# A two-part kernel, attention and a maxout feed-forward layer: its list of commands put in another order, with copies, casts and masks dealt to other engines

## The chip, the cores and the metric

The kernel runs on one core of a Trainium2 chip. The metric is device time in microseconds (us) of one execution. The core has a matrix engine (PE), a vector engine (DVE), an activation engine (ACT), a general one (POOL), and a fifth (SP) that here only issues transfers. Transfers go through 16 DMA engines, which the queues of SP, ACT and POOL share. In the profile, q0 carries what POOL issues, q1 what SP issues and q10 what ACT issues.

## The reference

Four batches, 8 heads, 768 positions, head size 64. Heads 0, 2 and 6 see all earlier positions ("far" heads); the other five see the first 4 positions and a window of 64 ("near" heads). The flags that say so are an input.

```
scores = q @ k.T / 8                      # (4, 8, 768, 768)
keep   = causal for heads 0, 2, 6; causal & (first 4 | last 64) for the others
a      = softmax(where(keep, scores, -1e9))
x      = (a @ v), heads side by side      # (3072, 512)
h      = max(x @ w1, x @ w2, x @ w3)      # 512 -> 768
out    = h @ w_out                        # 768 -> 512, fp32, (3072, 512)
```

All inputs are fp32; the kernel computes in fp16 and accumulates in fp32.

## The kernel before, in words

The kernel guesses the flags above, computes the fast path for them (`fast`, L154), compares the flags as it goes, and takes a general path at the end only if the guess was wrong or a sum is out of bounds.

The fast path has no loops over tiles. It is a list of commands, `PROGRAM` (L84), which the last lines of `fast` walk through in order, calling one small function for each. No scheduler reorders them: each engine gets its instructions in the order of the list and runs them in that order, waiting for others through semaphores. A command may put instructions on several engines. So the position of a command sets what stands behind what on each engine and on each queue, and a letter in it says which engine does its copy, cast or mask (a ACT, d DVE, p POOL, r a reduction on DVE) or which queue its transfer goes on (s SP, c or a ACT).

The stages of a batch, with their commands:

- **Batch 0 in.** Each half of 384 positions is loaded by pairs of heads: the first two pairs before the list begins, the rest by `hl half pair count queues` (L206, tiles `ks`, `qs`). `cast` turns k and q into fp16 (L220, `kn`, `qn`), `turnp` transposes them on PE (L238) and copies the result to `KQ` (L241). `load_v` loads v on SP's queue (L295 and L302, `vs`), `vc` casts it (L497), `vt` puts it in order by matmuls (L505) and copies it to `va` (L510). `kx0` and `y` copy the keys and values that near heads need beside the diagonal.
- **Batches 1 to 3 in.** `load b quad` loads k and q of four heads on POOL's queue (L257, `kq`), `turn` transposes them on DVE (L272). `load_v b half` on SP's queue, `v` and `y` cast v into place (L478, L524, L526).
- **Scores.** `s0` for batch 0 (L608), `s` for the others (L674): matmuls into a double bank `st`, then exponentials on ACT (L629, L691) to `pt`. `k0` and `k` multiply masks on (L377, POOL or DVE). A batch has 8 steps of `s`; they share two double banks.
- **Attention times v.** `av b half pair` (L717), reciprocal (L722) and product (L724) on DVE, then a transposing transfer on SP's queue (`D`, L730) or PE transposes and a copy (`x`, L740, L743) to `xT`.
- **Feed-forward.** `w 0` to `w 2` load w1 to w3 and `w 3` loads w_out, all on POOL's queue (L398, L393). `f b half wi ni` is one block of 128 of the 768 hidden columns with one of the three weights (L437, four matmuls): for wi 0 a copy to `acc` (L445), for wi 1 and 2 a maximum on DVE (L449). `o b half tb` is one block of 128 output rows (L462, six matmuls), a copy (L471) and a store (L472).
- **Others.** `gs` and `gp` are tiny transfers or copies that wait until something named has landed, and so hold back what is behind them on SP's queue or POOL. `idle` issues matmuls on zeros. `clear`, `cleark` fill constants. `flags`, `guess`, `check`, `verdict`, `read` compare the flags and sums and choose the path; `read` (L791) makes every engine load one value.

Buffers bound how far a command can run ahead: two of each tile of `hl` with two pairs, three `kq` tiles, three `vs` tiles, 17 tiles `pt`, four single and two double banks of PSUM.

The front of the list before, as far as POOL's and SP's queues go: on POOL `load 1 0`, `w 0`, `w 1`, `load 1 1`, `w 2`, `load 2 0`, each behind a number of copies and casts; on SP the k of `hl 0 2`, both halves of the first v, `hl 1 0`, `hl 1 2`, the second v.

The lines of `PROGRAM` that the prediction speaks of, before:

```
"turnp 1 0 dd, cast 1 3 dd, load 1 0, vt 0 02 da, cast 1 2 aa, vt 0 1 a, cast 1 1 pp",
"turnp 1 1 d, w 0, y 0 0 1:4:2 r p, s0 0 1 2, s0 0 1 3, y 0 0 4:5:1 r r, turnp 1 3 ad",
"turn 2 0 1 1, f 0 1 0 1 d, s 1 7, k 1 2 X 0 p, f 0 1 0 2 d, flags, load_v 1 0 s, v 1 0 0 d",
"w 3, v 1 0 2 d, f 0 1 1 2, s 1 3, f 0 1 2 2, f 0 1 1 1, load_v 1 1 s, k 1 3 Y 0 p, f 0 1 1 3",
"k 1 1 X 0 p, load_v 2 0 s, y 2 0 1:8:2 s a, f 0 1 1 5, f 0 1 2 5, y 1 1 1:8:2 r r",
```

Of the kernel before, what the change touches and what calls it, by code (L numbers as in the profile page):

```python
# [81 lines left out]
LEAST, MOST = 1.0e-9, 16.0  # L82

PROGRAM = (  # L84
# [65 lines left out]
)  # L150


# [889 lines left out]
```

## Time and profile before

| what | value |
|---|---|
| three runs | 192.91, 195.14, 195.88 us (median 195.14) |
| profiled execution, span | 195.2 us |
| PE busy | 180.9 us (93%) |
| DVE, ACT, POOL busy | 145.0, 98.8, 81.8 us |
| bytes moved | 26.59 MB |

The span runs from the first instruction to the end of the last transfer, and the profiled execution's own time is taken as that span. The shares are means over stages of different kinds: in the first third, where batch 0 is loaded and the scores of batch 0 and 1 are made, all engines and the transfers are busy; in the rest the feed-forward matmuls fill PE, and the others have room.

### The profile page before, as it was taken

How to read it: one execution, taken by the hardware profiler on the slowest of the kernel's cores; microseconds unless marked ns; L12 is line 12 of the kernel's file. 1: busy time of each engine (PE TensorE's matmuls, PEld its weight loads, DVE VectorE, ACT ScalarE, POOL GpSimd, SP SyncE). 2: the span in 40 equal slices, each digit the busy share in tenths (PEclk: the TensorE clock that was granted, in tenths of full speed). 3: DMA queues.
4: the chain of work that ended last, by engine and by line, in shares of the span. 5: the costliest groups of instructions: out<-in, count | busy, mean ns of one | idle time of the engine just before them, and what ended most of it. 6: DMA issues, size and time to landing. Idle time of an engine off the chain costs nothing.

```text
span 195.2 us, 4739 instructions
## 1 busy us (share of the span) xinstructions
PE 180.9 (93%) x1854; PEld 106.1 (54%) x1854; DVE 145.0 (74%) x308; ACT 98.8 (51%) x158; POOL 81.8 (42%) x140
## 2 busy tenths in 40 slices
PE   7896899998994899999999999999999999999990
PEld 2443646664562445675556565755665566565550
DVE  3758999987997393879897989857794689465541
ACT  3598797377944534679529532775434400211110
POOL 7595978819682296039705600332612500000000
PEclk9999999999999589999999999999999999999999
DMA  5999999999999647935969310241033012401413
GB/s 177 329 325 267 207 213 207 116 164 189 160 187 227 97 133 158 242 99 108 210 167 241 93 58 0 77 114 57 0 66 129 0 57 59 134 0 54 161 54 116
DMA packets 44248, 26.59 MB, mean 136 GB/s; under 512 B 31038, under 2 KB 39742, under 8 KB 44222
## 3 DMA queue, kind: packets, MB, share of 16 engines
q1 hardware_dynamic: 38798, 17.54, 36.8%
q0 software_dynamic: 4192, 7.87, 23.8%
q10 hardware_dynamic: 1232, 0.85, 1.4%
q8 instruction: 15, 0.25, 0.5%
q14 instruction: 11, 0.09, 0.1%
HBM read 25.17 MB, written 6.29 MB: 161 GB/s over the span
## 4 chain that ended last, share of the span: by engine, by line
PE 66%; DMA 12%; DVE 11%; SPq 5%; issue 2%; ACT 1%; ACTq 0%; DVEq 0%
PE yy L437 34%; PE yy L462 15%; DMA vs<-in_v_dram 8%; PE oacc L717 6%; PE st L674 5%; DMA qs<-in_q_dram 4%; SPq L302 4%; DVE KQ L272 4%; PE yst L437 3%; DVE x L724 2%; DVE acc L449 1%; PE yst L462 1%; DVE KQ L241 1%; SPq L283 1%; DVE vx L800 1%
## 5 line engine op out<-in xcount | busy, mean ns | idle before, releaser
L377 POOL TENSOR_TENSOR pt<-pt,kb 128x512 f16<-128x512 f16 (+5 forms) x53 | 48.3, 931 | 67.4 <-ACT pt L691 55.5
L691 ACT ACTIVATE pt<-st 128x1024 f16<-128x1024 f32 (+2 forms) x51 | 43.5, 908 | 24.6 <-PE st L674 24.2
L437 PE MATMUL yy<-xT,w2t 128*128 128x384 f16 x184 | 36.8, 330 | 0.0
L437 PE MATMUL yy<-xT,w0t 128*128 128x384 f16 x180 | 34.9, 326 | 0.6 <-DMA xT<-x 0.6
L437 PE MATMUL yy<-xT,w1t 128*128 128x384 f16 x176 | 34.4, 326 | 0.1
L462 PE MATMUL yy<-woutt,hT 128*128 128x512 f16 (+1 forms) x138 | 32.8, 384 | 0.0
L449 DVE TENSOR_TENSOR hT<-yy,acc 128x384 f16<-128x384 f32 x46 | 25.2, 555 | 6.8 <-PE yy L437 5.1
L449 DVE TENSOR_TENSOR acc<-yy,acc 128x384 f16<-128x384 f32 x44 | 24.0, 555 | 7.9 <-PE yy L437 4.0
L272 DVE STREAM_TRANSPOSE KQ<-kq 128x384 f32<-128x384 f32 x24 | 25.4, 1134 | 0.4 <-DMA kq<-in_q_dram 0.4
L437 PEld LDWEIGHTS <-w0t 128*128 128x128 f16 x192 | 18.1, 98 | 13.5 <-issue 1.7
L445 ACT CAST acc<-yy 128x384 f16<-128x384 f32 x27 | 12.9, 489 | 23.3 <-PE yy L437 21.2
L437 PEld LDWEIGHTS <-w1t 128*128 128x128 f16 x192 | 17.9, 98 | 12.3 <-issue 1.0
L437 PEld LDWEIGHTS <-w2t 128*128 128x128 f16 x192 | 17.8, 98 | 12.3 <-issue 0.9
L462 PEld LDWEIGHTS <-hT 128*128 128x128 f16 x150 | 14.8, 101 | 16.5 <-issue 2.0
L717 PE MATMUL oacc<-va,pt 128*128 128x65 f16 x392 | 19.1, 195 | 4.4 <-ACT va L478 3.5
L717 PEld LDWEIGHTS <-pt 128*128 128x128 f16 x472 | 17.6, 98 | 8.3 <-issue 4.4
L471 ACT COPY ot<-yy 128x512 f32<-128x512 f32 (+1 forms) x14 | 7.9, 566 | 23.6 <-PE yy L462 20.9
L724 DVE TENSOR_TENSOR x<-oacc,sums 128x384 f16<-128x384 f32 x32 | 17.8, 557 | 1.1
L629 ACT ACTIVATE pt<-st 128x1024 f16<-128x1024 f32 (+5 forms) x22 | 15.5, 760 | 3.1 <-PE st L608 2.9
L674 PE MATMUL st<-KQ 32*128 32x128 f16 (+2 forms) x342 | 15.3, 263 | 0.0
L377 DVE TENSOR_TENSOR pt<-pt,kb 128x256 f16<-128x256 f16 (+4 forms) x31 | 11.7, 383 | 1.8 <-ACT pt L691 1.7
L445 DVE CAST acc<-yy 128x384 f16<-128x384 f32 x18 | 10.0, 557 | 3.8 <-PE yy L437 3.3
(117 smaller groups left out, 187.6 us busy)
## 6 DMA issues: line engine op xcount, KB each, us to landing
out_dram<-ot SPq DMA_DIRECT2D x23, 256.0 KB, 2.2
vs<-in_v_dram SPq DMA_DIRECT2D x18, 256.0 KB, 6.0
ks<-in_k_dram SPq DMA_DIRECT2D x8, 192.0 KB, 5.1
kq<-in_k_dram POOLq DMA_DIRECT2D x3, 384.0 KB, 8.1
kq<-in_q_dram POOLq DMA_DIRECT2D x3, 384.0 KB, 9.2
kq<-in_k_dram POOLq DMA_DIRECT2D x3, 288.0 KB, 7.9
kq<-in_q_dram POOLq DMA_DIRECT2D x3, 288.0 KB, 10.0
qs<-in_q_dram ACTq DMA_DIRECT2D x4, 192.0 KB, 4.8
```

The costliest lines, as they stand in the source:

```text
L272: nc.vector.transpose(out=dst.rearrange("c (p j) -> c j p", j=n)[:, j0:j1], in_=src.rearrange("c (j i) -> c j i", i=R),)
L377: engine.tensor_tensor(out=x, in0=x, in1=of_blocks(kb, pattern, rows), op=ALU.mult)
L437: nc.tensor.matmul(yy[:, 0:HALF], w_t[wi][:, ks, ni * P : (ni + 1) * P], xT[b, half, ks].rearrange("p a t -> p (a t)"), start=(ks == 0), s ...
L445: op(out=acc[b, half, ni], in_=yy[:, 0:HALF])
L449: nc.vector.tensor_tensor(out=acc[b, half, ni] if wi == 1 else hT[b, half, ni], in0=yy[:, 0:HALF], in1=acc[b, half, ni], op=ALU.max,)
L462: nc.tensor.matmul(yo[:, 0:n], hT[b, half, ns][:, tb * P : (tb + 1) * P], woutt[:, ns, c : c + n], start=(ns == 0), stop=(ns == NNB - 1),)
L471: op(out=ot[:, c : c + n], in_=yo[:, 0:n])
L629: nc.scalar.activation(out=pts[0, half, hp, u][:, r0:r1, c0:c1], in_=sts[hp][:, r0:r1, c0:c1], func=AF.Exp, scale=sc,)
L674: nc.tensor.matmul(sts["XY"[g // 2]][:, g % 2, c0 : c0 + n * P], KQ[rows, 0, ki * P : (ki + 1) * P] if kind == "p" else kx[b % 2][quad][ro ...
L691: nc.scalar.activation(out=pts[b, s, xy][:, r0:r1, c0:c1], in_=st[:, r0:r1, c0:c1], func=AF.Exp, scale=sc,)
L717: nc.tensor.matmul(o[:, i, r, 0 : D + 1], at[b, h, kind, ki, qi], vv[:, 0 : D + 1], start=(n == 0), stop=(n == len(todo) - 1), skip_group_ ...
L724: nc.vector.tensor_tensor(out=x, in0=o[:, :, :, 0:D], in1=rc.unsqueeze(3).to_broadcast([P, HB, 2, D]), op=ALU.mult,)
```

## The change

Only `PROGRAM` changes. The same commands stand in another order, apart from the number of gates and idle matmuls, and in many of them the letter of the engine is another. The functions, tiles and buffers are untouched. What the prediction speaks of:

- POOL's first transfers: `load 1 0` stands behind the first cast, then `w 0`, `load 1 1`, `w 1`.
- SP's first transfers: `hl 0 2`, `hl 1 0`, the halves of the first v, the second v, and then `hl 1 2`.
- `load_v 1 1`, `1 0` and `2 0` and the gates that stood among them.
- `flags`, `guess`, `check`, `verdict` and `read` are near the end of the list.
- Letters: for instance the copies of `f` go from 28 on ACT and 20 on DVE to 31 and 17, the masks `k` from 43 on POOL and 29 on DVE to 45 and 27, copies of v (`v`) from 10 on ACT, 5 on DVE and 9 on POOL to 6, 4 and 10 and 4 reductions.

The front of the list, and the parts named (of 65 lines before and 68 after):

```diff
-    "idle 11, hl 0 2 2 sc, cast 0 1 pd, turnp 0 1 aa, cast 0 0 dd, cast 0 2 dp, load_v 0 0 0 4 s",
-    "load_v 0 0 4 4 s, turnp 0 0 ad, cast 0 3 pa, cleark 0 p, cleark 1 d, kx0 0 1 p, s0 0 1 1",
-    "s0 0 0 0, hl 1 0 2 ss, idle 1, turnp 0 3 da, turnp 0 2 da, s0 0 1 0, kx0 0 3 p, s0 0 0 3",
-    "vc 0 0 4 p, vc 0 4 4 p, s0 0 0 1, kx0 0 2 p, s0 0 0 2, hl 1 2 2 ss, cast 1 0 dd",
-    "turnp 1 0 dd, cast 1 3 dd, load 1 0, vt 0 02 da, cast 1 2 aa, vt 0 1 a, cast 1 1 pp",
-    "turnp 1 1 d, w 0, y 0 0 1:4:2 r p, s0 0 1 2, s0 0 1 3, y 0 0 4:5:1 r r, turnp 1 3 ad",
-    "s0 1 3 0, y 0 0 5:8:2 s r, clear 0 d, kx0 1 1 p, y 0 0 1:4:2 s p, s0 1 1 1, load_v 0 1 s",
-    "turnp 1 2 dd, kx0 1 2 r, av 0 0 1, s0 1 2 0, y 0 0 5:8:2 r r, kx0 1 3 r, w 1, gs 1, s0 1 0 1",
-    "av 0 0 0, av 0 0 3, s0 1 0 2, x 0 0 1 d, x 0 0 0 d, load 1 1, s0 1 3 2, vc 1 0 4 p",
+    "idle 11, cast 0 0 pd, load 1 0, hl 0 2 2 sc, turnp 0 0 aa, cast 0 3 dd, hl 1 0 2 ss",
+    "s0 0 0 0, w 0, cast 0 2 ap, load_v 0 0 0 4 s, turnp 0 2 ad, kx0 0 2 r, s0 0 1 2",
+    "cast 1 0 dd, cleark 0 p, turnp 0 3 da, load 1 1, turnp 1 0 ad, kx0 0 3 a",
+    "load_v 0 0 4 4 s, vc 0 4 4 d, vc 0 0 4 p, s0 0 0 3, s0 1 1 0, cast 0 1 pa, s0 1 0 0, w 1",
+    "load_v 0 1 s, vc 1 4 4 p, vt 0 1 a, s0 1 3 0, vt 0 02 da, y 0 0 1:4:2 s p, idle 1",
+    "vc 1 0 4 d, hl 1 2 2 ss, cast 1 2 ad, turnp 0 1 ad, vt 1 1 a, kx0 0 1 r, s0 0 1 3",
+    "cast 1 1 pp, turnp 1 1 a, cast 1 3 dd, s0 0 0 2, vt 1 02 da, y 0 0 4:5:1 s r, s0 0 1 0",
+    "turnp 1 2 ad, k0 0 0 2 d, y 0 1 1:4:2 r r, cleark 1 d, y 0 0 1:4:2 r d, y 0 0 4:5:1 r p",
+    "k0 0 3 2 d, y 0 0 5:8:2 s p, w 2, y 0 0 5:8:2 r a, s0 0 0 1, kx0 1 2 r, s0 0 1 1",
...
-    "k 1 1 X 0 p, load_v 2 0 s, y 2 0 1:8:2 s a, f 0 1 1 5, f 0 1 2 5, y 1 1 1:8:2 r r",
...
+    "k0 3 0 2 p, s 1 1, av 0 1 2 D, f 0 0 1 4, load_v 1 1 s, av 0 1 3, k 1 1 X 1 p, f 0 0 2 4",
+    "y 1 1 4:5:1 r p, s 1 2, k 1 2 X 1 p, k 1 1 Y 0 d, f 0 0 2 2, turn 2 0 0 0, x 0 1 3 a",
+    "f 0 0 2 1, k 1 2 X 0 d, f 0 0 2 5, s 1 3, k 1 3 X 0 p, f 0 1 0 5 a, f 0 1 1 5, clear 1 p",
+    "turn 2 0 1 1, load_v 1 0 s, y 1 1 1:8:2 r p, turn 2 0 0 1, kx 2 0 p, f 0 1 0 1 a",
+    "f 0 1 0 2 a, s 1 5, k 1 5 X 1 p, f 0 1 0 0 d, f 0 1 0 3 a, f 0 1 1 0, v 1 0 1 a",
+    "k 1 0 X 0 p, k 1 1 X 0 p, s 1 7, y 1 0 4:5:1 s p, f 0 1 2 0, k 1 5 X 0 p, w 3, f 0 1 1 1",
...
+    "load_v 2 0 s, v 2 0 1 a, f 0 1 2 4, v 2 0 0 p, gp 1 2, f 0 1 2 5, f 0 1 2 1, v 1 1 0 r",
...
+    "f 3 1 2 3, guess, verdict, f 3 1 1 1, f 3 1 2 1, o 3 0 0 a, f 3 1 2 4, f 3 1 2 5",
+    "o 3 1 1 d, o 3 1 0 d, o 3 1 2 a, read",
```

105 rows, old and new, of the table PROGRAM are left out of this document.

## The prediction

> **What bounds the kernel now.** I read the page first (busy shares, slices, the chain), then the table by stretches, then the chain in order of time, then the DMA queues of a few stretches.
>
> ```profile
> span 195.2 us, 4739 instructions
> PE 180.9 (93%) x1854; PEld 106.1 (54%) x1854; DVE 145.0 (74%) x308; ACT 98.8 (51%) x158; POOL 81.8 (42%) x140
> PEclk9999999999999589999999999999999999999999
> PE 66%; DMA 12%; DVE 11%; SPq 5%; issue 2%; ACT 1%; ACTq 0%; DVEq 0%
> 5.50:57.00 51.50, 46.49 (x554) 27.62 (x554) 44.66 (x90) 39.27 (x65) 37.60 (x72) 1.00 1.15 214
> 60.00:72.00 12.00, 8.50 (x65) 4.48 (x63) 7.73 (x14) 5.96 (x8) 4.87 (x8) 0.72 0.73 136
> 72.00:190.00 118.00, 118.00 (x1182) 70.15 (x1180) 87.18 (x189) 51.84 (x82) 32.68 (x45) 1.00 0.39 98
> ```
>
> The columns of a stretch are its length, then busy time of PE, PEld, DVE, ACT and POOL, then clock, DMA share and GB/s. From 72 to 190 PE has no gap at full clock. That part can only begin earlier or later: the change rearranges PE's work and takes none away. So a gain or a loss must lie in the first 72 us, and it has two places: 5 us missing of 51.5 in the front, and the hole at 60 to 72, which also halves the clock (the 5 in the slices).
>
> ```profile
> 51.10 10.15 DMA vs<-in_v_dram
> 61.28 1.04 ACT L526 CAST vx<-vs 64x1024 f16<-64x1024 f32 x1 [4.45 <-DMA vs<-in_v_dram]
> 64.17 0.65 PE L717 MATMUL oacc<-va,pt 128*128 128x65 f16 x9 [3.50 <-ACT va L478]
> ```
>
> The hole: a v transfer lands at 61.25, ACT, which takes its commands in order, is stuck 4.45 us at the cast that needs it, and PE waits 3.5 us for ACT's next cast of v. PE's mean clock over 60 to 72 is 0.72, which costs 12 x 0.28 = 3.4 us more, some of it beside the idle time: about 6.3 us in all.
>
> Why that v is late, and what the change could do to the front, is read from the queues (q0 carries what POOL issues, q1 what SP issues).
>
> ```profile
> q0 software_dynamic: 584, 0.60, 89.9%
> q1 hardware_dynamic: 572, 0.15, 27.6%
> vs<-in_v_dram SPq DMA_DIRECT2D x1, 256.0 KB, 15.7
> ...
> q0 software_dynamic: 336, 0.81, 104.6%
> q1 hardware_dynamic: 26, 0.02, 1.7%
> ...
> q1 hardware_dynamic: 680, 0.49, 110.4%
> ```
>
> The first three rows are 54 to 58 us, the next two 17 to 21, the last 12 to 13.5. Alone, SP's queue passes 680 packets in 1.5 us, 453 per us. When POOL's queue has work too (54 to 58), the two pass packets one for one, 584 to 572: SP's queue falls to 143 packets per us, a third, because POOL's packets are long. That is the wait on w 3 and `load 2 0`, and the 15.7 us of that v.
>
> **The change part by part.**
>
> *Engine shares.* Copies, casts and masks go to other engines, but by the durations of before's rows the sums stay: DVE 157.7 to 157.8 us, ACT 110.5 to 110.0, POOL 81.6 to 80.8, as I added them command by command. I take 0; in the stretch that is all PE they have room (DVE 87 of 118).
>
> *The v loads of batches 1 and 2.* The gates on SP's queue go to late places, `load_v 1 1`, `1 0` and `2 0` come one behind the other, and `w 3` behind the first two. The hole should not come back at this place: -6.3 us. If it does, the price is the same 6.3.
>
> *The tail.* `check`, `verdict`, `guess` and `read` move to the end. PE's last matmul ends at 190.50 and the span at 195.2; the 4.7 us are the last copy, store and its landing. `read` costs each engine one load of 0.3 to 0.6 us beside that: 0 to 0.6, I take 0.
>
> ```profile
> 190.50 0.03 ACTq L471
> L791 SPq TENSOR_LOAD <-differ x1: 592/592/592, 168.0 to 168.0; - x1
> ```
>
> *The front.* Here is the large term. Before, POOL issues `load 1 0` at 12.20, `w 0` at 14.44, `w 1` at 18.59 and `load 1 1` up to 21.4.
>
> ```profile
> 4.95 0.50 POOL L220 CAST kn<-ks 128x384 f16<-128x384 f32 x1 [0.54 <-DMA ks<-in_k_dram]
> ...
> 12.20 0.75 POOL L257 DMA_DIRECT2D kq<-in_k_dram  x1
> ...
> 18.59 0.75 POOL L398 DMA_DIRECT2D w1t<-in_moe_w_dram  x1
> ...
> 20.37 1.00 POOL L257 DMA_DIRECT2D kq<-in_q_dram  x2
> ...
> q0 software_dynamic: 34, 0.10, 52.6%
> kq<-in_q_dram POOLq DMA_DIRECT2D x1, 288.0 KB, 12.7
> 15.65 0.55 DVE L220 CAST qn<-qs 128x384 f16<-128x384 f32 x1 [0.59 <-DMA qs<-in_q_dram]
> ```
>
> The 34 packets are the whole of q0 in 16 to 17, and none came ahead of 16.2. So before, all of batch 0's q, k and v went out first with the DMA engines to itself (the last q is there at 15.65, SP's queue is all but empty at 17: 26 packets in 17 to 21), and the four POOL pieces ran behind it, from 16.2 to about 33.6 (the last issue at some 20.9 plus 12.7): 4.35 us each. After, `load 1 0` stands right behind the first cast (4.95 to 5.45), `w 0` and `load 1 1` follow with little before them, `w 1` behind the first cast of v; and SP's queue has the last q and k of batch 0 (`hl 1 2 2`) at its end, behind all of v. With one packet for one, whatever POOL's queue holds goes ahead of the end of SP's: from 8.9 (issue at 4.9 plus the 4.0 us from 12.20 to 16.2), SP's queue has 453 x (17.0 - 8.9) = 3670 packets left, POOL's four pieces some 1680 (the page has 4192 packets for ten such pieces).
>
> ```profile
> q0 software_dynamic: 4192, 7.87, 23.8%
> ```
>
> 3670 is over 1680, so all four pieces pass first and each sets the end of SP's queue back by its own 4.35 us: 17.0 + 4 x 4.35 = 34.4 for the last of `hl 1 2 2`, where its time without them is 17.0. The first of its four transfers lands some 1.8 us before (three quarters of 0.79 MB at 327 GB/s, the rate of the 12 to 13.5 stretch): 32.6. When POOL's queue starts hardly matters, as long as it starts before SP's is empty. `w 1` is the least sure: it waits for the first half of v, which is held back too (there at about 26), and it still goes ahead if SP's queue has over 420 packets left by then, which it has (3670 - 1257 = 2413 at the end of the third piece, 5.3 us alone, less some 3.5 us for v, its cast and the issue: about 815).
>
> What hangs on `hl 1 2 2`: ACT casts its first k in order, and everything of ACT stands behind it.
>
> ```profile
> L629 ACT ACTIVATE pt<-st 128x1024 f16<-128x1024 f32 (+5 forms) x22 | 15.5, 760 | 3.1 <-PE st L608 2.9
> L691 ACT ACTIVATE pt<-st 128x1024 f16<-128x1024 f32 x39 | 38.3, 1021 | 20.1 <-PE st L674 19.9
> ```
>
> From that cast up to `s 1 2`, ACT has 15 of batch 0's 22 exponentials (10.7 us), 6 of batch 1's (6 x 1.02 = 6.1) and 20 casts and copies (11.1), 27.9 us. DVE has 27 there, so ACT sets it. The last two exponentials are behind PE's part, so PE is through `s 1 2` at 32.6 + 27.9 - 2.0 = 58.5. Then PE's own work is left: 131 hidden blocks, 24 output blocks, 21 score steps and three batches of attention times v.
>
> ```profile
> 111.39 8.45 PE yy L437 x52
> 178.80 3.88 PE yy L462 x18
> 121.13 0.56 PE st L674 x12
> 123.47 1.31 PE oacc L717 x42
> ```
>
> Four matmuls are a hidden block: 8.45 / 13 = 0.65, 131 x 0.65 = 85.2. Six are an output block: 3.88 / 3 = 1.29, 24 x 1.29 = 31.1. Score steps 21 x 0.565 = 11.9. Attention 118 matmuls a batch, 3 x 118 x 0.031 = 11.0. Together 139.2. With 2.0 for short waits and the tail's 4.7, the **sum is 58.5 + 139.2 + 2.0 + 4.7 = 204.4**. It is made against the profiled 195.2, which stands on the median, 195.14. In general, with n POOL pieces ahead of `hl 1 2 2`, the time is 187.0 + 4.35 n. I take n = 4 and round to 204. The waits, 2.0, I don't see in the trace: 0 if DVE and POOL never lag, 5 (what PE lacks of 51.5 in before's front) if they do as before.
>
> ```profile
> 12.00:14.00 2.00, 2.00 (x25) 1.23 (x26) 1.08 (x4) 1.91 (x3) 1.95 (x6) 1.00 1.09 324
> ```
>
> The 4.0 us from 12.20 to 16.2 are the one thing that speaks for another start. In those 4 us DVE ran casts of fp32, up to 16.20. The Trainium skill, SBUF — State Buffer, "🔬 SBUF: two separate sides", says that a POOL-issued transfer's descriptors can't be written while DVE runs a copy in its two-port mode, fp32 copies above all. By that rule the start would be at the end of DVE's early casts, some 9.5 in after, which would leave the sum as it is and take the ground from rival B; the trace agrees in the one start at 16.2, but DVE was busy for only 1.08 of the 2 us from 12 to 14, so it doesn't prove it.
>
> **The rivals.**
>
> *B, faster, n = 0 to 1.* POOL's queue gets going only as SP's runs dry. For it: before's first POOL packet comes at 16.2, just as SP's queue empties. Against it: at 54 to 58 the two queues do share, while SP's was far from empty. What decides: whether POOL's packets start before 15 or not. Then `hl 1 2 2` is there at 15.2 to 17, the front runs as in before or better, and the hole at 61 is gone: 187.0 to 191.4, I take 189. It checks from the other end: 195.2 less the 6.3 of the hole is 188.9.
>
> *C, no change, n = 2.* POOL's queue shares but starts late (after 12) or runs dry, since `load 1 1` and `w 1` stand behind casts of data that is itself held back; two pieces go ahead: 195.7. The gain of the hole and the loss in front are then about equal. For it: `w 1` hangs on v; against it: nothing holds `load 1 0` and `w 0`, and `load 1 1` waits only for the cast of a q on the first loads.
>
> *D, slower by less, n = 3.* `w 1` comes too late to go ahead: 200.1.
>
> *E, slower by more.* As forecast, and the hole comes back with some other v: 204.4 + 6.3 = 210.7. Against it: the v loads have no gate and no weight in their way.
>
> **How the numbers follow.** Forecast (n = 4) 0.38, own range 201 to 208; D 0.12; B 0.28; C 0.18; E 0.04. Faster by over 2% (below 191.2) is B, 0.28. Slower by over 2% (above 199.0) is the forecast, D and E less a little, since D lies on the bound: 0.52. Within 2%, about what a measurement of this kernel tells from no change: 0.20. The range of 8 in 10 goes from B's middle to the top of the forecast, 188 to 208.
>
> **What would show it.** Right: in the stretch 8 to 26, q0 and q1 have equal packet counts and the GB/s that SP's queue moves fall to a fifth; the cast of batch 0's last q is past 30 (15.65 before); PE's slices from 12 to 33 us show low digits and the clock falls; no wait of ACT for v at 61; PE solid from 58 to 199. Wrong: q0 without packets before 15 (B); the last cast at 24 to 26 (C) or near 29 (D). The forecast also falls if PE, though late, has less than 139 us left then, because other blocks were done in the wait: the order on PE is fixed, so I hold that for unlikely.

## The result, and the profile after

The changed kernel takes **226.7 us** (median of five runs, 223.7 to 228.7) against 195.1 for before (median of five, 191.4 to 200.3). The ratio is **1.17, 95% interval 1.148 to 1.193**. The forecast had the sign and not the size: 204.

Both kernels have some longer executions, the profiled ones of before (span 195.2) and after (span 226.9) among them, and every ratio here is made between the others, where before takes 190.2 to 191.0 us on the chips of the experiments.

Where a difference in us is given below, the ratio is multiplied by about 190.4. The changed kernel is then at 222.9, and its interval alone runs from 218.6 to 227.2. A run's time is 1.7 to 2.1 us longer than its span. The prediction's sum is one of spans.

The page of the changed kernel:

```profile
span 226.9 us, 4743 instructions
PE 189.1 (83%) x1854; PEld 108.5 (48%) x1854; DVE 155.1 (68%) x302; ACT 99.8 (44%) x162; POOL 81.4 (36%) x142
PE   7405296899999858759995999999999999999980
PEclk9955569799999988958999799999999999999996
PE 52%; DVE 17%; DMA 16%; SPq 5%; ACT 4%; issue 3%; DVEq 0%; ACTq 0%
```

PEld is PE's loading of weights. Each of the 40 slices is 5.7 us. PE has three weak places. The first is the front (slices 2 to 5, 6 to 28 us, with the clock at half from slice 3 on), the second runs from slice 14 to 18 (74 to 102 us) with the clock down again, the third is slice 22 (119 to 125 us). DVE, which had 11% of the chain before, has 17% now.

The front, first the queues from 12 to 16 us, then the casts of batch 0's v and of its last keys and queries, then PE at `s 1 2` (line numbers are 3 higher than before):

```profile
q0 software_dynamic: 379, 0.62, 84.0%
q1 hardware_dynamic: 377, 0.27, 27.6%
```

```profile
25.16 0.82 POOL L500 CAST vn<-vs 128x768 f16<-128x768 f32 x1 [14.23 <-DMA vs<-in_v_dram]
...
30.67 0.51 ACT L223 CAST kn<-ks 128x384 f16<-128x384 f32 x1
...
32.88 0.55 DVE L223 CAST qn<-qs 128x384 f16<-128x384 f32 x1
...
59.47 0.22 PE L677 MATMUL st<-KQ 32*128 32x128 f16 x4
```

One packet for one, 379 to 377, as the prediction read it from 54 to 58 us of before. POOL gets its first v at 25.2 (forecast: about 26), ACT's first cast of the last k is at 30.7 (32.6), the last q is cast at 32.9 (34.4), and `s 1 2` ends on PE at 59.7 (58.5). In these numbers the forecast holds within 2 us. The way there is another one, as the queues from 25 to 30 us, q1 from 30 to 36 and two pieces of the chain show:

```profile
q1 hardware_dynamic: 1747, 1.28, 85.4%
q0 software_dynamic: 123, 0.19, 24.6%
...
q1 hardware_dynamic: 11, 0.01, 0.4%
...
8.23 18.07 DMA vs<-in_v_dram
26.33 0.57 DVE vn L500
```

POOL issues `w 1` at 26.38, and by 30, when SP's queue has 11 packets left, only 123 packets of POOL's queue have passed, of some 420 in a piece. So three pieces went ahead of SP's queue and the fourth came too late, as in rival D. The chain runs through the v transfer, and no piece of it is a transfer of `hl 1 2 2`.

Behind it, by stretches (length, busy PE, PEld, DVE, ACT, POOL, clock, DMA share, GB/s), and the pieces of the chain in the weak place:

```profile
59.70:220.40 160.70, 149.20 (x1426) 86.28 (x1426) 122.82 (x229) 65.65 (x100) 53.10 (x93) 0.96 0.47 102
80.00:99.00 19.00, 11.78 (x127) 6.35 (x123) 17.08 (x21) 4.15 (x6) 10.50 (x16) 0.86 0.92 165
```

```profile
81.97 7.51 DVE pt L380
...
92.55 6.40 DMA xT<-x
```

PE's last matmul ends at 220.4, that is 160.7 us after `s 1 2`, where the forecast had 139.2 and 2.0 for waits. PE stands idle for 11.5 us of these, and the other 10.0 above 139.2 are in its busy time, at a mean clock of 0.96. In 80 to 99 alone PE is busy for 11.8 of 19 us. The chain goes through one DVE instruction of 7.51 us. The timelines of DVE and of POOL show what it is:

```profile
81.42 0.56 DVE L727 TENSOR_TENSOR x<-oacc,sums 128x384 f16<-128x384 f32 x1
81.89 7.60 DVE L380 TENSOR_TENSOR pt<-pt,kb 128x128 f16<-128x128 f16 x1
89.41 0.18 DVE L725 RECIPROCAL sums<-oacc 128x6 f32<-128x6 f32 x1
...
118.00 4.11 DVE L380 TENSOR_TENSOR pt<-pt,kb 128x1024 f16<-128x1024 f16 x2
```

```profile
80.02 3.50 POOL L380 TENSOR_TENSOR pt<-pt,kb 128x512 f16<-128x512 f16 x4
83.47 0.49 POOL L481 CAST va<-vs 128x384 f16<-128x384 f32 x1
83.93 1.77 POOL L380 TENSOR_TENSOR pt<-pt,kb 128x256 f16<-128x256 f16 x2
85.66 0.94 POOL L481 CAST va<-vs 128x384 f16<-128x384 f32 x2
86.57 2.39 POOL L380 TENSOR_TENSOR pt<-pt,kb 128x256 f16<-128x256 f16 x3
88.92 0.49 POOL L481 CAST va<-vs 128x384 f16<-128x384 f32 x1
```

A mask of 128x128 (`k 1 4 X 0`), 0.23 us elsewhere, takes 7.60 us and ends at 89.49, just as POOL's row of masks and casts ends at 89.41. The same again at 118: the first of the two masks (`k 2 2 Y 0`) lasts 3.85 us, until 0.6 us after POOL's next row ends. Before the row at 80 us POOL stood still at a copy of v, and its work then comes without a gap (read from the trace, not tried by itself). It also issues `w 3` late, and PE waits for w_out:

```profile
67.68 0.29 POOL L527 CAST vx<-vs 64x128 f16<-64x128 f32 x1 [8.67 <-DMA vs<-in_v_dram]
...
82.95 2.33 PE L465 MATMUL yy<-woutt,hT 128*128 128x512 f16 x6 [2.53 <-DMA woutt<-in_moe_w_out_dram]
```

So there were three theories of the 32 us: the late front, the long masks, and the order behind the front as such.

### The profile page after: what moved, and what is told of

Read it like the earlier page. It is cut to its first block, busy times and chain, and to the rows that moved or that the text cites. A ratio compares the mean times of both kernels' runs of the same rounds, so it can differ in the third digit from the quotient of the medians.

```text
span 226.9 us, 4743 instructions
## 1 busy us (share of the span) xinstructions
PE 189.1 (83%) x1854; PEld 108.5 (48%) x1854; DVE 155.1 (68%) x302; ACT 99.8 (44%) x162; POOL 81.4 (36%) x142
## 4 chain that ended last, share of the span: by engine, by line
PE 52%; DVE 17%; DMA 16%; SPq 5%; ACT 4%; issue 3%; DVEq 0%; ACTq 0%
PE yy L440 27%; PE yy L465 10%; DMA vs<-in_v_dram 10%; DVE pt L380 6%; DMA xT<-x 4%; SPq L305 4%; PE st L677 3%; PE oacc L720 3%; DVE x L727 3%; PE yst L440 3%; DMA ks<-in_k_dram 2%; DVE hT L452 2%; DVE acc L452 2%; PE vb L508 2%; ACT pt L632 1%
## 5 line engine op out<-in xcount | busy, mean ns | idle before, releaser
L380 POOL TENSOR_TENSOR pt<-pt,kb 128x256 f16<-128x256 f16 (+5 forms) x53 | 46.5, 896 | 53.0 <-ACT pt L694 42.6
L465 PE MATMUL yy<-woutt,hT 128*128 128x512 f16 (+1 forms) x138 | 34.1, 393 | 4.7 <-DMA woutt<-in_moe_w_out_dram 2.5
L440 PE MATMUL yy<-xT,w1t 128*128 128x384 f16 x184 | 36.9, 331 | 0.0
L440 PE MATMUL yy<-xT,w2t 128*128 128x384 f16 x184 | 36.0, 326 | 0.7 <-DVE hT L452 0.5
L452 DVE TENSOR_TENSOR acc<-yy,acc 128x384 f16<-128x384 f32 x46 | 25.2, 554 | 14.8 <-PE yy L440 11.9
L474 ACT COPY ot<-yy 128x512 f32<-128x512 f32 (+1 forms) x16 | 9.1, 566 | 49.7 <-PE yy L465 35.5
L380 DVE TENSOR_TENSOR pt<-pt,kb 128x512 f16<-128x512 f16 (+5 forms) x31 | 25.1, 823 | 3.9 <-ACT pt L694 3.8
L440 PEld LDWEIGHTS <-w0t 128*128 128x128 f16 x192 | 18.0, 99 | 17.1 <-DMA xT<-x 4.1
L720 PEld LDWEIGHTS <-pt 128*128 128x128 f16 x472 | 19.1, 101 | 7.4 <-issue 1.7
L720 PE MATMUL oacc<-va,pt 128*128 128x65 f16 x392 | 20.9, 199 | 1.8 <-DVE pt L380 1.5
L677 PEld LDWEIGHTS <-KQ 32*128 32x128 f16 x342 | 9.3, 95 | 7.7 <-issue 6.6
```

Of the source, the lines that this page charges most:

```text
L380: engine.tensor_tensor(out=x, in0=x, in1=of_blocks(kb, pattern, rows), op=ALU.mult)
L440: nc.tensor.matmul(yy[:, 0:HALF], w_t[wi][:, ks, ni * P : (ni + 1) * P], xT[b, half, ks].rearrange("p a t -> p (a t)"), start=(ks == 0), s ...
L452: nc.vector.tensor_tensor(out=acc[b, half, ni] if wi == 1 else hT[b, half, ni], in0=yy[:, 0:HALF], in1=acc[b, half, ni], op=ALU.max,)
L465: nc.tensor.matmul(yo[:, 0:n], hT[b, half, ns][:, tb * P : (tb + 1) * P], woutt[:, ns, c : c + n], start=(ns == 0), stop=(ns == NNB - 1),)
L474: op(out=ot[:, c : c + n], in_=yo[:, 0:n])
L677: nc.tensor.matmul(sts["XY"[g // 2]][:, g % 2, c0 : c0 + n * P], KQ[rows, 0, ki * P : (ki + 1) * P] if kind == "p" else kx[b % 2][quad][ro ...
```

## The experiments

**The front, taken out and put in alone.** In the changed kernel, POOL's four first loads were moved behind its last cast of batch 0:

```diff
-cast 0 0 pd, load 1 0, ...   s0 0 0 0, w 0, ...   turnp 0 3 da, load 1 1, ...   s0 1 0 0, w 1
+cast 1 1 pp, load 1 0, w 0, load 1 1, w 1
```

> The changed kernel with one part undone: load 1 0, w 0, load 1 1 and w 1 stand behind the last cast that POOL does of batch 0 (cast 1 1), so that batch 0's q, k and v have the queues to themselves. Theory (POOL's early loads starve batch 0): the first cast of the last k is back from 30.67 to 16 to 18 us, PE is through s 1 2 at 43 to 46 instead of 59.7, and the time falls by 13 to 16 us to 208 to 212; more, down to 192, if the waits of PE between 70 and 128 were a consequence of the late front. Rival (the order of the list itself is bad and the loads are hidden): under 4 us gained, 219 or more.

Measured: 214.4 us, ratio 1.126 (1.123 to 1.129). The last q is cast at 20.2, and all behind it comes 11 us sooner, the 7.6 us mask as well (at 71.0 now). The gain is 8.5 us from 222.9. That is less than the front costs by itself (17.1, in h2_front_of_after below). A wait that the edit makes of its own, 3.1 us on PE, is a part of the difference. The rest stays open.

The reverse, in the kernel before:

```diff
-cast 1 3 dd, load 1 0, ...   turnp 1 1 d, w 0, ...   kx0 1 3 r, w 1, ...   x 0 0 0 d, load 1 1
+cast 0 1 pd, load 1 0, ...   cleark 0 p, load 1 1, ...   s0 0 0 0, w 0, ...   vc 0 0 4 p, w 1
```

> The kernel before with that part alone: load 1 0 behind the first cast, load 1 1 and w 0 a few commands on, w 1 behind the first cast of v. Theory: three to four pieces of 4.35 us go ahead of hl 1 2, the last k and q of batch 0 are cast at 28 to 33 instead of 15.65, and the time is 205 to 212. Rival (the starved data is not what the front hangs on, or the queues don't share there): 193 to 198, or a little faster since batch 1 is there sooner.

Measured: 207.5 us, ratio 1.090 (1.083 to 1.096), **17.1 us** more. The queues from 20 to 26 us, and the last q:

```profile
q0 software_dynamic: 616, 0.92, 84.0%
q1 hardware_dynamic: 617, 0.45, 30.3%
...
31.50 0.55 DVE L223 CAST qn<-qs 128x384 f16<-128x384 f32 x1 [1.18 <-DMA qs<-in_q_dram]
```

It is 15.85 us later than the 15.65 of before. Here `w 1` is issued at 14.46, so that all four pieces go ahead, and the time is close to the forecast's 4 x 4.35 = 17.4. With two of the four pieces:

```diff
-cast 1 3 dd, load 1 0, ...   turnp 1 1 d, w 0
+cast 0 1 pd, load 1 0, w 0
```

> The kernel before with only load 1 0 and w 0 moved to the front, w 1 and load 1 1 where they were. The prediction's price of 4.35 us for each piece ahead of hl 1 2: two pieces, so 8.7 us over before, and the last q of batch 0 cast at 24 instead of 15.65. If the price isn't per piece (a fixed loss once POOL's queue has begun), 15 us or more; if the two fit in beside SP's queue, under 3.

Measured: ratio 1.039 (1.026 to 1.051), 7.4 us more, the last q at 22.76. The price is by the piece.

**The two long masks.** Two letters of the changed kernel:

```diff
-k 1 4 X 0 d   k 2 2 Y 0 d
+k 1 4 X 0 p   k 2 2 Y 0 p
```

> The changed kernel with two letters changed: the masks k 1 4 X 0 and k 2 2 Y 0, which took 7.60 and 3.8 us on DVE while POOL ran without a gap, go to POOL. Theory (DVE's masks are locked out by POOL's run): DVE has 7.3 and 3.2 us back, the two holes of PE at 83 to 99 and 118 to 127 shrink, and 5 to 9 us are gained, 216 to 220. Rival (POOL's own queue of masks and casts of v sets the end there anyway): under 2 us, 223 to 226.

Measured: ratio 1.129 (1.123 to 1.135), some **8 us** less than the changed kernel (about 4 us either way, by the two intervals). No DVE mask is over 1.7 us there, and PE has 15.69 busy us from 80 to 99 where it had 11.78. But at the second place a DVE copy of keys (`kx`, 128x512, 0.28 us elsewhere) now takes 2.99 us.

```profile
80.00:99.00 19.00, 15.69 (x185) 9.28 (x185) 11.96 (x25) 8.58 (x13) 11.66 (x18) 0.91 1.00 176
```

**Both.** The edits of e1_pool_late and e3_two_masks together:

> The changed kernel with both undone: POOL's first loads late as in e1_pool_late, and the two masks on POOL as in e3_two_masks. If the two costs are separate, they add: 214.4 less some 8, so 205 to 208. If the masks only matter in the starved schedule: 213 to 215.

Measured: 206.9 us, ratio 1.078 (1.062 to 1.093): they add, 17.7 us under the changed kernel by the ratios, for 8.5 and 8 of the two alone. But 15 us over before are left, and a third mask takes 3.55 us. It is the one of 128x384, `k 2 1 X 0`. (The expectations of e10_spaced_w3 and h3_front_of_before_masks call it `k 2 3 Y 0`, which is a mask of 128x256 and takes 0.46 us here.) Part of the rest is the edit's own: POOL issues loads in a row from 19.2 on, the second transfer of the last one (`load 2 0`) waits 3.2 us until the first weight has landed, and PE waits for constants that stand in that row.

```profile
25.80 0.33 POOL L387 MEMSET va<- 128x48 f16 x1
25.87 0.35 POOL L388 MEMSET vx<- 128x20 f16 x1
26.52 0.54 POOL L260 DMA_DIRECT2D kq<-in_k_dram  x1 [0.31 <-DMA kq<-in_q_dram]
30.24 0.54 POOL L260 DMA_DIRECT2D kq<-in_q_dram  x1 [3.17 <-DMA w0t<-in_moe_w_dram]
...
26.18 0.44 PE L720 MATMUL oacc<-va,pt 128*128 128x65 f16 x9 [3.19 <-POOL va L387]
```

So the loads were spaced out:

```diff
-cast 1 1 pp, load 1 0, w 0, load 1 1, w 1
+vc 1 4 4 p, load 1 0, ...   cast 1 1 pp, w 0, clear 0 p, ...   y 0 0 4:5:1 r p, w 1, ...
+y 0 0 5:8:2 s p, load 1 1, ...   k0 0 1 2 p, w 2, ...   k0 1 1 2 p, load 2 0
```

> As e6_both, but POOL's first loads are spaced out: load 1 0 behind the last cast of v, w 0 behind the last cast of k and q, then the constants of va, then w 1, load 1 1, w 2 and load 2 0 with copies and masks between. In e6_both they stood in a row, POOL issued loads from 19.2 to 26.8, and PE waited 3.2 us for the constants at half clock behind it. Theory (that wait was made by the placement alone): 3 to 6 us less than e6_both, 201 to 204. Rival (the front is bound by ACT): less than 2 us.

Measured: 205.3 us, ratio 1.063 (1.043 to 1.083). The interval touches that of e6_both; the wait for the constants is gone, but PE has no more busy time up to 57 us than there (43.37 us, against 43.24). No DVE mask is over 1.7 us in it, and some 12 us over before are left all the same.

**What is left behind the front.** Two tries at single waits:

```diff
 e7_both_v_early, from e6_both
-load_v 1 1 s, load_v 1 0 s       (behind f 0 0 1 4, and behind turn 2 0 1 1)
+s0 1 1 3, load_v 1 1 s, load_v 1 0 s
 e10_spaced_w3, from e9_spaced
-w 3                              (behind k 1 5 X 0 p)
+kx 2 0 p, w 3
-k 2 3 Y 0 d
+k 2 3 Y 0 p
```

> The same as e6_both, and load_v 1 1 and load_v 1 0 are moved ahead, behind the last scores of batch 0, so that they don't wait on SP's queue behind the transposing transfers of av 0 1. Theory (POOL stands 8.7 us at a copy of v, gets a backlog of 20 us, and w 3, DVE's masks and PE's av pay for it): the 8.7 us wait goes, w_out lands before PE needs it, and 4 to 10 us more are gained, 196 to 203. Rival (the order of PE's and POOL's other work holds those stretches): less than 2 us against e6_both.

> As e9_spaced, with w 3 ahead on POOL (behind kx 2 0) and the third long mask (k 2 3 Y 0, 3.55 us in e6_both) on POOL. PE waits for w_out 2.1 us and for DVE 2.3 us in e6_both, each with a time at half clock behind it: 4 to 7 us less than e9_spaced, 195 to 199. Rival (another wait stands right behind each): less than 2 us.

Measured: ratios 1.079 (1.057 to 1.101) and 1.084 (1.074 to 1.095), no gain over their bases. POOL's 8.7 us wait for v is gone in the one and PE's wait for w_out in both. In their place stand others. In e10_spaced_w3 PE waits 3.4 us for DVE's maximum (`acc`) and 2.6 us for a product of batch 0. The mask that this edit moves was not the long one, so the third long mask stays on DVE, at 2.0 us. And in front of that `acc` a `kx` copy takes 3.30 us on DVE (3.18 in e7_both_v_early, where PE waits 2.1). As the rivals said, another wait stood behind each.

**The list cut in two.** The commands of before up to `s 1 0` with the rest in the changed order (h1), and the changed list up to its `s 1 0` with the rest in before's order (h2):

> The list of before up to its first score step of batch 1 (s 1 0), and behind it all commands that are left, in the order and with the letters of the changed list. The front costs nothing more then. Theory (the late front costs some 14 to 17 us, the order behind it the other half, 7 to 8 of it by the locked masks): 202 to 208, and one or more DVE masks of over 3 us. Rival (the waits behind the front are a consequence of the late front): 190 to 195.

> The reverse: the changed list up to its s 1 0, and behind it all that is left in the order of before. Theory: the late front alone, 14 to 18 us over before, 205 to 209, with no DVE mask over 1.2 us. Rival (the front's loss is made up later, or it is the combination that costs): under 200.

Measured: h1 199.3 us, ratio **1.046** (1.041 to 1.052), 8.8 us over before. h2 207.3 us, ratio **1.090** (1.082 to 1.097), 17.1 us over before. These two and the masks add up to the whole: 17.1 + 8.8 + 8 = 33.9, where 222.9 - 190.4 = 32.5 was measured. With 4 us either way on the last of the three, this agrees, and it does not prove that the parts are independent.

In h2 PE has 33.59 busy us from 5.5 to 57 at a clock of 0.80, and from 80 to 190 it has no gap, as in before. In h1 the front is sound, and the largest wait of PE, 2.9 of the 8.8 us, stands at one place, where PE's output blocks wait for DVE (the stretch, the wait, and what DVE and POOL do there):

```profile
90.00:100.00 10.00, 7.08 (x97) 4.47 (x97) 9.12 (x15) 4.91 (x10) 6.03 (x9) 1.00 0.74 125
...
PE yy L465 <- DVE acc L452: 2.9, 1, 2.9
...
92.23 3.23 DVE L578 COPY kx<-KQ 128x32 f16<-128x32 f16 x1
...
92.70 1.18 POOL L380 TENSOR_TENSOR pt<-pt,kb 128x512 f16<-128x512 f16 x1
93.80 0.52 POOL L481 CAST va<-vs 128x384 f16<-128x384 f32 x1
94.26 1.16 POOL L380 TENSOR_TENSOR pt<-pt,kb 128x512 f16<-128x512 f16 x1
```

I had expected a mask of over 3 us in h1, and none is over 1.7. But a `kx` copy of 128x32, 0.16 us elsewhere, takes 3.23 us there, right before the `acc`, and ends at 95.46 as POOL's row ends at 95.42. So a part of the order's 8.8 us is a held DVE instruction as well, and it need not be a mask. This row of POOL, a mask, a cast and a mask behind `load 3 1`, holds some DVE instruction in most kernels with the changed order: a mask in the changed kernel, e1_pool_late and e6_both, a copy in e3_two_masks, e7_both_v_early, e10_spaced_w3 and h1. The letters of the masks decide which one. With them on POOL:

```diff
-k 1 4 X 0 d   k 2 2 Y 0 d   k 2 3 Y 0 d
+k 1 4 X 0 p   k 2 2 Y 0 p   k 2 3 Y 0 p
```

> As h1_front_of_before, with the three masks that were long (k 1 4 X 0, k 2 2 Y 0, k 2 3 Y 0) on POOL. Theory: 7 to 9 us less than h1_front_of_before, 195 to 200. Rival (other masks are locked in their place, or POOL's own row is then as late): under 3 us.

Measured: 202.0 us, ratio 1.062 (1.055 to 1.069), 3 us slower than h1. My expectation was wrong. The row still holds DVE: a `kx` copy takes 3.29 us and the mask of 128x384 2.03, and PE waits 3.4 us for the same `acc`.

**The hole at 60 to 72 us.** The prediction counted 6.3 us for it. `w 3` out of the way of the v loads, and before once more as it is:

```diff
 e4_before_w3_late
-f 0 1 0 0 d, w 3
+load_v 2 0 s, w 3
```

> The kernel before with w 3 moved behind load_v 2 0, so that the v loads of batches 1 and 2 don't share with it. The prediction's term for the hole at 60 to 72: -6.3 us, 187 to 191. Rival (another transfer, load 2 0 or the gates, holds v as well, or w_out is then late): 193 to 197.

> The kernel before, unchanged, for a second trace. The prediction took the hole at 60 to 72 us (6.3 us) as a part of every execution. If so, it is here again. If it is a mark of the longer executions, this trace has PE nearly full from 57 to 72 at a span near 189.

Measured: 191.0 and 191.4 us for the executions of e4_before_w3_late that are compared, against 189.8 to 190.4 for before: no gain. The second trace of before has a span of 189.2, and its stretches show no hole:

```profile
60.00:72.00 12.00, 11.78 (x99) 5.85 (x96) 9.83 (x16) 5.87 (x10) 9.04 (x14) 1.00 1.25 209
```

PE has 11.78 of 12 us, at full clock, where the first trace had 8.50 at 0.72. The hole belongs to the one execution that the first profile had caught, and not to the kernel's order.

**What holds the masks.** Short stretches behind the last output of before, in which DVE gets one mask (in e5_probe a product of 128x64, or a copy) beside a row of POOL's work:

```diff
+first POOL instruction, on which DVE's mask depends
+    then: 2, 8, 16 products of 128x128 | 8 copies | 8 fills            (e5_probe)
+    then: 8 masks of 128x512 | 8 of 2x128 | 8 casts | the row of eleven (e11_probe_masks)
+    the same behind two loads on POOL's queue                           (e12_probe_loads)
+    a load is issued first, so that DVE's mask has begun                (e13_probe_begun)
```

> The kernel before, with six short stretches behind its last output: POOL runs 2, 8 or 16 products of two 128x128 fp16 tiles one behind the other (0.42 us each), or 8 copies, or 8 fills, and DVE gets one product of 128x64 that is ready when POOL's first is done; in the last stretch a copy. Theory (DVE can't get in as long as POOL's instructions follow without a gap): the DVE product takes about as long as POOL's run, 0.8, 3.4 and 6.7 us for 2, 8 and 16. Rival (it waits for one POOL instruction at most, and the 7.60 us were something else): 0.6 us or less in all stretches.

> The kernel before with four stretches behind its last output, nearer to the case than e5_probe: POOL runs 8 masks of 128x512, 8 of 2 x 128, 8 casts of v, or the row of eleven masks and casts that ran beside the 7.60 us mask, and DVE gets one 128x128 mask that is ready when POOL's first instruction is done. If a row of POOL's work shuts DVE out, one of the stretches shows a DVE mask of 3 us or more, and tells which instructions do it. If not, all are under 1.3 us, and what made the 7.60 us stays open.

> As e11_probe_masks, with two loads of w_out on POOL's queue issued ahead of each stretch, since the long masks of the changed kernel came while transfers that POOL had issued were under way (8 masks of 128x512; the row of eleven; three masks and then the row; 8 casts). If POOL's transfers under way are what shuts DVE out behind POOL's row, a DVE mask here takes 3 us or more. If all stay under 1.3 us, that isn't it either, and the cause of the 7.60 us stays open.

> Like the probes before, but now DVE's mask (four stretches with 128x1024, the last with 128x128) is ready while POOL issues a load, so that it has begun when POOL's row of masks and casts begins, as it was with the 3.85 us mask of the changed kernel. If a mask that has begun is held by each POOL instruction that follows, it takes 3 us or more here. If it takes under 2 us in all five, the cause stays open.

Measured: in none of 19 stretches is a DVE instruction over 1.7 us. The plainest one, of e11_probe_masks:

```profile
187.95 9.76 POOL L380 TENSOR_TENSOR pt<-pt,kb 128x512 f16<-128x512 f16 x8
...
188.02 1.16 DVE L380 TENSOR_TENSOR pt<-pt,kb 128x128 f16<-128x128 f16 x1 [0.36 <-POOL pt L800]
```

DVE's mask waits for the POOL mask that is running (some 1 us), then it gets in, though seven more follow. Beside casts it takes 0.49, and e5_probe's product takes 0.24 beside copies and 0.19 beside fills. So what makes a DVE instruction wait through a whole row, ten instructions at 81.9, stays **open**. That a mask does, the same one in two kernels (7.60 and 7.58 us), and that taking the two masks off DVE gains some 8 us, is shown.

## Why the prediction was wrong

- **POOL's loads go ahead of batch 0, packet for packet: right, but three of them and not four.** 379 to 377, and 616 to 617. The price of 4.35 us a piece measured 17.1 for four in e2_before_pool_early (forecast 17.4) and 7.4 for two (8.7). In the changed kernel `w 1` was too late. The working let it go ahead if SP's queue had over 420 packets left. But its own packets began some 2 us behind the issue at 26.38, and at 28.5 SP's queue had 227 left. That queue ran dry at about 30.3, where 17.0 + 3 x 4.35 gives 30.05.
- **What hangs on `hl 1 2 2`, 27.9 us of ACT: right in the number, by luck in part.** `s 1 2` ended at 59.7, forecast 58.5. ACT's first cast of k came 1.9 us before its forecast, and 29.0 us passed from it to the end of `s 1 2` where the forecast had 25.9. In these 29.0 ACT was busy for 22.9 us and PE for 26.3, so ACT alone did not set them, and the chain before them runs through v.
- **The step that failed is "PE's own work is left", 139.2 us and 2.0 for waits.** It measured 160.7, with 11.5 us of PE idle and 149.2 busy. The quoted bounds of that term were 0 to 5 us, taken from before's front, and the text held that the part of PE without a gap "can only begin earlier or later", since the change takes none of PE's work away. Two things stood against it and were not worked out. First, behind `s 1 2` the order is another one, and alone it costs 8.8 us (h1): the masks, maxima and transposes that PE waits for come from in-order DVE and POOL, and I added up their work without asking what stands in front of each on its engine. Second, POOL and DVE meet in other places, and an instruction of DVE is then held through a row of POOL's: some 8 us for two masks in the changed kernel, which in h1, with the same order behind a sound front, take no longer than usual (there the 3.23 us copy is held, inside the 8.8). The 118 us without a gap in before were the result of its order, and not a floor that PE's work gives.
- **The hole, -6.3 us: wrong as a term of the change.** Before without any change is 6.0 us shorter in its second trace. The hole went into the sum through the base of 187.0, a span, which lies 2.2 us below the 189.2 of the trace without the hole (e8_before_again). It had been read from one execution, and the range of the three runs (192.9 to 195.9) was the warning.
- **The engine shares, 0: wrong in kind.** The prediction added up work, but the engine of two masks mattered by 8 us in the changed kernel (moved to POOL, they gain), and by 3 us the other way in h3.
- **Rivals.** B (faster) fell at its own test: q0's first packets came between 7 and 7.5 us, long before 15, while SP's queue was at work (145 packets in that half us). D had the number of pieces right, three, but not the time, 200.1. E had the right idea, that a wait behind the front returns, with 210.7 and a chance of 0.04. The range ended at 208 since each term had been bounded from before's trace, and no term had the order behind the front.
- **The rule of the Trainium skill, SBUF — State Buffer, "🔬 SBUF: two separate sides", on POOL's descriptors:** the start came some 2.4 us after the issue at 4.83, with DVE idle from 4.72 to 8.24, against 4.0 with DVE's casts beside it in before. This agrees with the rule, and no run here tests it. The Trainium skill, SBUF — State Buffer, "Who interferes with whom", says that a DVE instruction with two inputs in SBUF and a POOL instruction that reads SBUF shut each other out, and that the one which comes first keeps the other waiting for one whole instruction. The probes agree (1.16 us); the 7.60 us mask doesn't, and there the measurement decides.

## What to carry to other kernels

A transfer that is issued earlier on a second queue is not free: count what waits in the other queues at that time, and price each piece that goes ahead by its own time. Where engines run their lists in order, equal sums of work say nothing about the waits: walk, for each command that the main engine waits for, what stands before it on its engine, and do it with the times that the front gives, since a shift of one engine against another makes new meetings. And take no stall from one trace for a term before a second execution shows it. If an instruction of one engine is held, look at the whole engine and not at that group alone: with the masks moved away, a copy was held in their place.

## What the runs showed of the hardware

- A DVE product of two SBUF tiles took 7.60, 7.58, 3.85, 3.55 and 2.98 us beside rows of POOL's work, ending within 0.6 us of the row's end each time. A DVE copy between SBUF tiles took 2.99 us (e3_two_masks), 3.18 (e7_both_v_early), 3.23 (h1), 3.29 (h3) and 3.30 (e10_spaced_w3), where 0.16 to 0.28 is usual; the first three end within 0.2 us of the row's end, the last two about 0.2 us behind the row's first mask. In isolated rows a product waited for one POOL instruction (1.16 us). The difference was not found.
- POOL's own issue of a load came late once more was under way: after five loads and the first half of the sixth, the next transfer was issued 3.17 us late, when the first weight had landed (e6_both).
- SP's queue, at 453 packets per us alone, passes some 91 per us beside POOL's queue in the changed kernel (731 in 12 to 20 us), a fifth.

```profile
q0 software_dynamic: 733, 1.29, 85.9%
q1 hardware_dynamic: 731, 0.53, 26.5%
```
